# A dynamic convolution with a top-1 mixture of experts: PSUM tiles of three banks become tiles of two banks and of one, with a new order of the steps

## The chip, the core and the metric

The kernel runs on one core of a Trainium2 chip, with five engines: PE (TensorE, matmuls), DVE (VectorE), ACT (ScalarE), POOL (GpSimd) and SP (SyncE, here a queue of DMA issues). The metric is device time in microseconds of one execution; the median of three is quoted. TensorE's clock has two levels, 1.2 and 2.4 GHz; the profile gives the granted clock of a stretch as a share of the full one.

## What is computed

The reference has two stages. The first is a convolution whose seven weights per head come from a softmax of `weight_gen`; the second sends each row to the one expert with the largest logit.

```python
# batch 8, seq 3584, d_model 192, 8 heads of 24, K = 7
w = softmax(weight_gen, axis=-1)                       # [8, 3584, 8, 7]
x_pad = np.concatenate([zeros(8, 6, 192), x], axis=1)
out[b, s, h, g] = sum_k w[b, s, h, k] * x_pad[b, s + k, h, g]
# 28672 rows of 192; E = 8 experts, F = 1024
logits = out @ w_gate + modality_bias[modality_id]
e = argmax(logits); p = softmax(logits)[e]
y = p * (relu(out @ w1[e]) @ w2[e])
```

## The kernel before

**Units and pages.** The first stage works on 16 units u: 8 batches times 2 halves. A unit has 14 tokens on each of the 128 partitions, in two chunks c of 7 tokens, so a tap (one of 7 weights times the shifted x) is an operation on 128x1344. The second stage works on pages of 256 rows that belong to one expert (128 rows for the last five): 5 pages after unit 0, 7 after each later unit, 115 in all. After a unit's rows are known its gate, its route (which page and place each row gets) and the scatter of its rows to HBM follow; pages then load rows by expert.

**A page.** Rows and weights are held as two f16 parts (`hi` and `lo`). `page_h` (HM, L1021) makes half of the 1024 hidden columns at a time: two groups of 20 matmuls 128x256, each into 1024 f32 columns of PSUM. `page_hi` (HA, L1033, ACT) writes relu of it as f16, `page_lo` (HL, L1037, DVE) the remainder. `page_out` (OM, L1050 to L1052) makes the second product for half a page: 24 matmuls 128x192, which read both groups' `hi` and `lo` (tile `hl`). `page_store` (OA, L1057, ACT) scales that output by the gate's weight into `ot`, `page_scatter` (OS, L1062, POOL) sends it to `out`. `page_scale` (GM, L1006) prepares the scale.

**A unit.** `softmax_exp` (X, L532, ACT), sums on DVE, then `softmax_n` (BN, L562, DVE) writes the chunk's normalised weights `wn`, 392 columns, into PSUM. Each `tap` (PQ, L568, DVE) reads `wn` and writes a product, which `add` (PA, L619, DVE), `add_far` (DA, L614, an adding DMA that POOL issues) and `merge` (PM, L623) sum up. Units 0 and 1 take another way: `product` (M, L580) on DVE and `tap_sum` (S, L597), which sums on PE with an identity into a PSUM accumulator. `rows_hi` (H, L629, ACT) and `rows_lo` (L, L637 and L638, DVE) split the sum into f16 parts. `bias_rows` (XB, L536, ACT) copies the gate's bias for modality 0, `token_bias` (BP, L547, DVE) puts in that of modality 1. The gate's weights are prepared once: `gate_bound` (L432, DVE), `gate_parts` (L441 to L447) with `place` (L421).

**PSUM.** Two tiles hold nearly everything, `banks[0]` and `banks[1]`, three banks (1536 f32 columns) each. Columns 0 to 1023 take h: group 0 of each page in `banks[0]`, group 1 in `banks[1]`. The last bank of `banks[0]` takes the outputs of OM, its two halves by turns; the last bank of `banks[1]` takes `wn`. For units 0 and 1 a whole tile is the accumulator. Waits between engines are put in by the framework, which sees tiles.

**The order.** The program is one list, the string ORDER, of 3614 tokens such as `HM.45.0` (step, page or unit, part). Each token's step is issued in that order, so the list fixes the order on every engine's queue.

Of the kernel before, what the change touches and what calls it, by code (L numbers as in the profile page):

```python
# [1171 lines left out]
```

## Time and profile before

| what | value |
|---|---|
| median of 3 runs (lowest, highest) | 1463.68 us (1463.45, 1466.26) |
| the profiled execution | 1476.15 us |
| its span | 1474.4 us |
| busy: PE, DVE, ACT, POOL | 1186.4, 1018.2, 605.6, 575.3 us |
| mean granted clock of TensorE | 0.931 |

The span goes from the first to the last instruction of the one profiled execution; the rest of that execution's time lies around it. Busy time is the union of an engine's instructions. An engine's idle time is put down to the event that ended it (the releaser). Instructions are named by line and by tile: `hl<-banks` on L1037 reads a PSUM tile and writes `hl`.

### The profile page before, as it was taken

What the parts mean: (1) busy time and instruction counts of PE and PEld (TensorE: products, weight loads), DVE (VectorE), ACT (ScalarE), POOL (GpSimd) and SP (SyncE); (2) the same over time, 40 slices, a digit from 0 to 9 for tenths busy, and PEclk for the clock granted to TensorE, in tenths of its full rate; (3) what the DMA queues carried; (4) which work ended last, traced back from release to release, by engine and by line L of the source; (5) the groups of instructions that cost most, each with busy time, mean ns of one, the idle gap of its engine ahead of it and who ended that gap; (6) DMA issues with size and microseconds to landing.
All of it is one profiled execution on the core that took longest, in us unless ns stands there. A gap on an engine that the chain in (4) does not pass through costs nothing. (4 is left out here: it accounts for less than half of the span.)

```text
span 1474.4 us, 30152 instructions
## 1 busy us (share of the span) xinstructions
PE 1186.4 (80%) x11625; PEld 1035.1 (70%) x11625; DVE 1018.2 (69%) x1225; ACT 605.6 (41%) x1051; POOL 575.3 (39%) x566
## 2 busy tenths in 40 slices
PE   7587677788788888888878887888788888878884
PEld 3345566677777777777777777777677877768883
DVE  5687788887778786778867676678677878442210
ACT  3766353534435453534334362354234333323321
POOL 2151524352262625253534435126352534433111
PEclk8789889999999999999999899899899999989997
DMA  9577654796354565635464633548676463742122
GB/s 300 179 260 232 165 137 123 207 284 152 71 144 83 154 151 152 132 85 152 100 173 95 180 87 78 147 84 194 119 167 162 97 130 79 165 119 63 39 78 66
DMA packets 200630, 206.02 MB, mean 140 GB/s; under 512 B 157088, under 2 KB 173724, under 8 KB 195489
## 3 DMA queue, kind: packets, MB, share of 16 engines
q1 hardware_dynamic: 170720, 120.50, 30.8%
q0 software_dynamic: 29760, 83.53, 23.9%
q8 instruction: 93, 1.52, 0.4%
q14 instruction: 57, 0.47, 0.1%
HBM read 262.81 MB, written 57.95 MB: 218 GB/s over the span
## 5 line engine op out<-in xcount | busy, mean ns | idle before, releaser
L1021 PE MATMUL banks<-xT,w 128*128 128x256 f16 (+1 forms) x4600 | 548.2, 276 | 59.4 <-DVE hl L1037 18.7
L1050 PE MATMUL banks<-w,hl 128*128 128x192 f16 x1800 | 466.0, 259 | 153.9 <-DVE hl L1037 104.2
L1021 PEld LDWEIGHTS <-w 128*128 128x128 f16 x4600 | 448.0, 100 | 124.9 <-issue 49.5
L1062 POOL DMA_INDIRECT out_dram<-ot,meta x225 | 251.8, 1119 | 634.3 <-ACT ot L1057 391.2
L1052 PE MATMUL banks<-w,hl 128*128 128x192 f16 x1800 | 467.3, 260 | 3.4 <-DVE hl L1037 3.4
L1051 PE MATMUL banks<-w,hl 128*128 128x192 f16 x1800 | 467.1, 259 | 0.0
L1037 DVE SCALAR_TENSOR_TENSOR hl<-banks,hl 128x1024 f16<-128x1024 f32 x225 | 273.5, 1219 | 202.6 <-ACT ot L1057 107.8
L1033 ACT ACTIVATE hl<-banks 128x1024 f16<-128x1024 f32 x225 | 229.4, 1020 | 295.3 <-PE banks L1052 134.5
L743 POOL DMA_INDIRECT rows_scratch<-rows,idx x224 | 253.5, 1132 | 148.0 <-ACT rows L738 77.0
L1051 PEld LDWEIGHTS <-hl 128*128 128x128 f16 x1800 | 185.7, 103 | 175.2 <-issue 171.9
L568 DVE TENSOR_TENSOR shared<-banks,xt 128x1344 f32<-128x1344 f32 x140 | 216.4, 1550 | 80.1 <-PE banks L1021 72.1
L1057 ACT ACTIVATE ot<-banks,gm 128x192 f32<-128x192 f32 x225 | 93.6, 418 | 387.2 <-PE banks L1021 275.1
L1050 PEld LDWEIGHTS <-hl 128*128 128x128 f16 x1800 | 185.6, 103 | 10.2 <-ACT hl L1033 6.6
L1052 PEld LDWEIGHTS <-hl 128*128 128x128 f16 x1800 | 186.4, 104 | 6.7 <-DVE hl L1037 4.5
L619 DVE TENSOR_TENSOR shared<-shared 128x1344 f32<-128x1344 f32 x84 | 129.9, 1546 | 0.7
L568 DVE TENSOR_TENSOR prod<-banks,xt 128x1344 f32<-128x1344 f32 x56 | 86.8, 1551 | 36.4 <-PE banks L1021 33.1
L614 POOL DMA_DIRECT2D shared<-prod x56 | 54.0, 972 | 79.5 <-DVE prod L568 70.9
L597 PE MATMUL banks<-prod,ident 128*128 128x512 f32 x144 | 66.6, 616 | 20.9 <-DVE prod L580 13.6
L651 ACT ACTIVATE xg<-gt 128x768 f16<-128x768 f16 x84 | 67.6, 805 | 29.3 <-PE gt L647 28.6
L597 PEld LDWEIGHTS banks<-prod,ident 128*128 128x128 f32 x144 | 29.9, 216 | 53.5 <-issue 36.9
L647 PE MATMUL gt<-ident,rows 128*128 128x128 f16 x504 | 45.6, 226 | 23.1 <-ACT xg L651 11.8
L503 ACT ACTIVATE junk<-xt 128x1920 uint8<-128x1920 f32 x32 | 57.5, 1797 | 0.8 <-DMA xt<-in_x_dram 0.6
(142 smaller groups left out, 742.3 us busy)
## 6 DMA issues: line engine op xcount, KB each, us to landing
w<-weights_scratch SPq DMA_DIRECT2D x115, 1280.5 KB
w<-weights_scratch SPq DMA_DIRECT2D x230, 256.0 KB
shared<-prod POOLq DMA_DIRECT2D x56, 672.0 KB
xt<-in_x_dram SPq DMA_DIRECT2D x15, 1920.0 KB
weights_scratch<-w SPq DMA_DIRECT2D x8, 1280.5 KB
wt<-in_weight_gen_dram SPq DMA_DIRECT2D x16, 392.0 KB
out_dram<-ot,meta POOLq DMA_INDIRECT x225
rows_scratch<-rows,idx POOLq DMA_INDIRECT x224
```

The lines of the kernel that those rows point to most:

```text
L568: return nc.vector.tensor_tensor(to.rearrange("p t (h g) -> p t h g", h=H), win, xin, ALU.mult)
L597: nc.tensor.matmul(un[u]["psum", c][:, q], lhsT=ident32, rhs=un[u]["pr", c, k][:, q], start=(k == order[0]), stop=(k == order[-1]))
L619: return nc.vector.tensor_tensor(a, a, un[u]["tmp"], ALU.add)
L743: i = nc.gpsimd.indirect_dma_start(out=rows, out_offset=bass.IndirectOffsetOnAxis(ap=idx[:, j:j + 1], axis=0), in_=ri[:, j, 0:ROW // 2], i ...
L1021: nc.tensor.matmul(o, lhsT=wt[:, w0:w0 + P], rhs=xT[:, xi, :pt], start=(q * pt % 512 == 0 and j == 0), stop=(j == 4), skip_group_check=True)
L1033: return nc.scalar.activation(hi, pg["ps", grp], AF.Relu)
L1037: return nc.vector.scalar_tensor_tensor(lo, live[i]["ps", grp], 0.0, hi, op0=ALU.max, op1=ALU.subtract)
L1050: nc.tensor.matmul(ps, lhsT=hi, rhs=wt[:, w0:w0 + D], start=(f == 0), stop=False)
L1051: nc.tensor.matmul(ps, lhsT=hi, rhs=wt[:, w0 + D:w0 + 2 * D], start=False, stop=False)
L1052: nc.tensor.matmul(ps, lhsT=lo, rhs=wt[:, w0:w0 + D], start=False, stop=(f == NFT - 1))
L1057: nc.scalar.activation(ot, pg["out", t], AF.Copy, scale=pg["gm"][:, t:t + 1])
L1062: w = nc.gpsimd.indirect_dma_start(out=out, out_offset=bass.IndirectOffsetOnAxis(ap=pg["meta"][:, t, 1:2], axis=0), in_=pg["res", t], in_o ...
```

## The change

The three-bank tiles are replaced by `pairs[0..1]` (1024 columns, two banks) for h, and `singles[0..1]` (512 columns, one bank): `singles[0]` takes the outputs, its two halves at columns 0 and 256, `singles[1]` takes `wn`. Eight banks are laid out as before. The accumulator of units 0 and 1 is split: its first 5 tokens (WIDE) are in a pair, the last 2 in a single, so H and L run as two parts each, and `tap_sum` cuts its three matmuls at 512 and 960 columns. The seven operations of `gate_parts` run on DVE. The token `XB.0` goes from second place to behind `SA.0.1`, and ORDER is another one: the same tokens, of which 2245 stand in other places. The diff, cut; of ORDER it shows the first line and the place of `BN.9.0`, of before and of the change:

```diff
-ORDER = """A.0 XB.0 TE.0 RI.0 RI.1 wld.0 X.0 SM.0 CL SN.0 B.0 WP SA.0.0 M.0.0.0 M.0.0.1 S.0.0.0 SA.0.1 M.0.0.2 wld.1 CC S.0.0.1 SB.0
...
-PA.8.1.6 OA.42.1 SC.7.13 PW.46 HL.44.0 GM.46 OM.43.0 HA.44.1 OS.41.1 BN.9.0 BP.9 HL.44.1 OS.42.0 HM.45.0 OA.43.0 PQ.9.0.0
...
+ORDER = """A.0 RI.0 TE.0 RI.1 wld.0 X.0 SM.0 CL SN.0 B.0 WP SA.0.0 M.0.0.0 M.0.0.1 S.0.0.0 SA.0.1 M.0.0.2 wld.1 CC S.0.0.1 XB.0 SB.0
...
+OM.42.1 PA.8.1.6 LU.10 XB.10 OS.41.1 HA.43.1 SC.7.9 HL.43.1 HM.44.0 OA.42.1 PW.46 GM.46 BN.9.0 SC.7.10 PQ.9.0.0 SC.7.11
+OM.43.0 HA.44.0 PQ.9.0.1 OS.42.0 HM.44.1 HL.44.0 OA.43.0 SC.7.12 PQ.9.0.3 SC.7.13 OM.43.1 HA.44.1 PQ.9.0.4 OS.42.1 HL.44.1
...
-        wn = un[u]["wn", c] = banks[1][:, 1024:1024 + n * H * K].rearrange("p (t h k) -> p t h k", h=H, k=K)
+        wn = un[u]["wn", c] = singles[1][:, 0:n * H * K].rearrange("p (t h k) -> p t h k", h=H, k=K)
...
-            un[u]["psum", c] = banks[turn_of("acc", 2)]
-            un[u]["acc", c] = un[u]["psum", c][:, :n * D].rearrange("p (t d) -> p t d", d=D)
-        for j in range(0, n * D, 512):
-            q = slice(j, min(j + 512, n * D))
-            nc.tensor.matmul(un[u]["psum", c][:, q], lhsT=ident32, rhs=un[u]["pr", c, k][:, q], start=(k == order[0]), stop=(k == order[-1]))
+            q = turn_of("acc", 2)
+            un[u]["psum", c] = pairs[q], singles[q]
+            un[u]["acc", c] = [(0, WIDE, pairs[q][:, 0:WIDE * D].rearrange("p (t d) -> p t d", d=D)),
+                               (WIDE, n, singles[q][:, 0:(n - WIDE) * D].rearrange("p (t d) -> p t d", d=D))]
+        wide, rest = un[u]["psum", c]
+        for to, a, z in ((wide, 0, 512), (wide, 512, WIDE * D), (rest, WIDE * D, n * D)):
+            o = 0 if to is wide else WIDE * D
+            nc.tensor.matmul(to[:, a - o:z - o], lhsT=ident32, rhs=un[u]["pr", c, k][:, a:z], start=(k == order[0]), stop=(k == order[-1]))
...
+    def pieces(u, c):
+        acc = un[u]["acc", c]
+        return acc if isinstance(acc, list) else [(0, CHUNKS[c][1], acc)]
...
-        nc.scalar.activation(ri.bitcast(F16)[:, :, 0:D], un[u]["acc", c], AF.Copy, scale=un[u]["sx"])
+        for a, z, acc in pieces(u, c):
+            nc.scalar.activation(ri.bitcast(F16)[:, a:z, 0:D], acc, AF.Copy, scale=un[u]["sx"])
...
-        ps = pg["ps", grp] = banks[turn_of("g1", 2)][:, 0:1024]
+        ps = pg["ps", grp] = pairs[turn_of("g1", 2)]
...
-        o = 1024 + 256 * pool["turn"]
-        ps = pg["out", t] = banks[0][:, o:o + D]
+        o = 256 * pool["turn"]
+        ps = pg["out", t] = singles[0][:, o:o + D]
...
-    banks = [psg.tile([P, 3 * 512], F32, name=f"banks{q}") for q in range(2)]
+    pairs = [psg.tile([P, 1024], F32, name=f"pair{q}") for q in range(2)]
+    singles = [psg.tile([P, 512], F32, name=f"single{q}") for q in range(2)]
```

`rows_lo` loops over `pieces` in the same way, and `place` and `gate_parts` differ only in `nc.vector` for `nc.gpsimd`.

What the change does to the queues is seen in three places. The first is DVE around the weights of unit 8, chunk 0 (L562 before, L563 now; taps are L568 and L569, `hl` is L1037 and L1048). Each row is an instruction with the semaphores that it waits for. Before:

```order
L562 TENSOR_TENSOR banks1_167<-wt_5853,sm_7010 128x392 [waits DVE_49,Activation_49]
L1037 SCALAR_TENSOR_TENSOR hl_160<-banks1_167,hl_160 128x1024 [waits DVE_49]
L568 TENSOR_TENSOR shared_171<-banks1_167,xt_5852 128x1344 [waits DMAHW5_49]
L568 TENSOR_TENSOR prod_7114<-banks1_167,xt_5852 128x1344
L568 TENSOR_TENSOR shared_171<-banks1_167,xt_5852 128x1344
L568 TENSOR_TENSOR shared_171<-banks1_167,xt_5852 128x1344 [waits PE_49]
L1037 SCALAR_TENSOR_TENSOR hl_160<-banks0_166,hl_160 128x1024 [waits PE_49,Activation_49]
L1037 SCALAR_TENSOR_TENSOR hl_160<-banks1_167,hl_160 128x1024 [waits Activation_49]
L619 TENSOR_TENSOR shared_171<-shared_171 128x1344 [waits DVE_49]
L568 TENSOR_TENSOR prod_7219<-banks1_167,xt_5852 128x1344 [waits DMASW6_49]
L623 TENSOR_TENSOR shared_171<-shared_171 128x1344 [waits DMASW2_49]
L568 TENSOR_TENSOR shared_171<-banks1_167,xt_5852 128x1344 [waits DVE_49,PE_49]
```

and now:

```order
L563 TENSOR_TENSOR single1_169<-wt_5841,sm_6752 128x392
L569 TENSOR_TENSOR shared_173<-single1_169,xt_5840 128x1344 [waits DMAHW5_49,DVE_49]
L569 TENSOR_TENSOR prod_7037<-single1_169,xt_5840 128x1344
L1048 SCALAR_TENSOR_TENSOR hl_160<-pair0_166,hl_160 128x1024 [waits Activation_49]
L569 TENSOR_TENSOR shared_173<-single1_169,xt_5840 128x1344 x2
L1048 SCALAR_TENSOR_TENSOR hl_160<-pair1_167,hl_160 128x1024 [waits Activation_49]
L623 TENSOR_TENSOR shared_173<-shared_173 128x1344 [waits DVE_49]
L569 TENSOR_TENSOR prod_7160<-single1_169,xt_5840 128x1344 [waits DMASW4_49]
L1048 SCALAR_TENSOR_TENSOR hl_160<-pair0_166,hl_160 128x1024 [waits Activation_49]
L569 TENSOR_TENSOR shared_173<-single1_169,xt_5840 128x1344 [waits DVE_49]
L1048 SCALAR_TENSOR_TENSOR hl_160<-pair1_167,hl_160 128x1024 [waits Activation_49]
```

The taps read `single1` and wait for no matmul; `hl` waits for ACT alone; one `hl` stands after each tap or two.

The second is the start of ACT's queue, with the bias copy (`bt`), the first exponential (`wt`) and the two sums over x (`junk`). Before:

```order
L536 ACTIVATE bt_219<-bias_86 128x112 [waits DMAHW0_49]
L757 ACTIVATE tb_221<-ee0_152 1x4 [waits Pool_49]
L632 ACTIVATE rows0_72<-ids_130 128x14
L632 ACTIVATE rows1_73<-ids_130 128x14
L532 ACTIVATE wt_75<-wt_75 128x784 [waits DVE_49]
L543 ACTIVATE sm_229<-sm_229 128x112 [waits DVE_49]
L503 ACTIVATE junk_237,asum_236<-xt_74 128x1920 [waits DMAHW3_49,DMAHW2_49,DMAHW1_49]
L503 ACTIVATE junk_246,asum_236<-xt_74 128x1920 [waits DMAHW5_49,DMAHW6_49,DMAHW4_49,Activation_49]
```

and now:

```order
L641 ACTIVATE rows0_72<-ids_130 128x14 [waits Pool_49]
L768 ACTIVATE tb_222<-ee0_152 1x4 [waits Pool_49]
L641 ACTIVATE rows1_73<-ids_130 128x14
L533 ACTIVATE wt_75<-wt_75 128x784 [waits DMAHW0_49,DVE_49]
L544 ACTIVATE sm_229<-sm_229 128x112 [waits DVE_49]
L504 ACTIVATE junk_237,asum_236<-xt_74 128x1920 [waits DMAHW3_49,DMAHW2_49,DMAHW1_49]
L504 ACTIVATE junk_246,asum_236<-xt_74 128x1920 [waits DMAHW5_49,DMAHW6_49,DMAHW4_49,Activation_49]
L537 ACTIVATE bt_266<-bias_86 128x112 [waits DMAHW0_49]
```

The copy has moved from the head of the queue to behind the two sums.

The third is the preparation of the gate's weights. Before, in POOL's queue, up to the DMA that adds the far tap of unit 0:

```order
L441 TENSOR_SCALAR gate_ex_110<-gate_max_109 128x1 [waits DVE_49,Pool_49]
L442 TENSOR_SCALAR gate_ex_110<-gate_ex_110 128x1 [waits Pool_49]
L421 TENSOR_SCALAR gate_sb_111<-gate_ex_110 128x1 [waits Pool_49]
L421 TENSOR_SCALAR gate_sb_111<-gate_ex_110 128x1
L445 TENSOR_SCALAR wgf_107<-wgf_107,gate_sb_111 128x48 [waits Pool_49]
L446 CAST wg_112<-wgf_107 128x6x8 [waits Pool_49]
L447 TENSOR_TENSOR wg_112<-wgf_107,wg_112 128x6x8 [waits Pool_49]
L614 DMA w_3_164<-prod_318 128x1344 [waits DVE_49]
```

and now, in DVE's queue, between the gate's bound and the next product:

```order
L433 TENSOR_REDUCE gate_max_109<-w_3_164 128x1 [waits DMAHW6_49]
L442 TENSOR_SCALAR gate_ex_110<-gate_max_109 128x1 [waits DVE_49]
L443 TENSOR_SCALAR gate_ex_110<-gate_ex_110 128x1 [waits DVE_49]
L422 TENSOR_SCALAR gate_sb_111<-gate_ex_110 128x1 [waits DVE_49]
L422 TENSOR_SCALAR gate_sb_111<-gate_ex_110 128x1
L446 TENSOR_SCALAR wgf_107<-wgf_107,gate_sb_111 128x48 [waits DVE_49,Pool_49]
L447 CAST wg_112<-wgf_107 128x6x8 [waits DVE_49]
L448 TENSOR_TENSOR wg_112<-wgf_107,wg_112 128x6x8 [waits DVE_49]
L581 TENSOR_TENSOR w_3_164<-xt_74,wt_75 128x1344 [waits DMAHW5_49,DMAHW4_49]
```

POOL's queue goes from the copies of the gate's weights (L439) straight to that DMA.

## Rows read from the trace of the kernel before

**Rows 1.** The view by stretches, with its line of columns, four of six stretches.
```profile
core 0: us, PE busy (x) PEld busy (x) DVE busy (x) ACT busy (x) POOL busy (x), PEclk, DMA share, GB/s
0.00:121.00 121.00, 88.48 (x339) 43.99 (x339) 84.71 (x97) 65.46 (x110) 39.17 (x75) 0.84 0.71 234
121.00:298.00 177.00, 130.18 (x1275) 112.78 (x1274) 146.99 (x170) 93.13 (x155) 66.67 (x60) 0.91 0.64 180
298.00:1302.00 1004.00, 832.17 (x8576) 754.29 (x8575) 742.22 (x890) 402.82 (x709) 425.90 (x386) 0.95 0.57 134
...
1340.00:1420.00 80.00, 70.22 (x721) 63.99 (x719) 20.22 (x17) 23.75 (x41) 15.48 (x16) 1.00 0.26 64
```

**Rows 2.** Waits of PE, 298 to 1302 us: us in total, times, longest us.
```profile
PE banks L1050 <- DVE hl L1037: 81.8, 57, 2.8
PE banks L1050 <- ACT ot L1057: 38.0, 63, 3.1
PE banks L1021 <- DVE hl L1037: 13.1, 10, 1.4
PE banks L1021 <- DVE shared L568: 9.0, 11, 2.1
```

**Rows 3.** Waits of ACT and DVE, 298 to 1302 us.
```profile
ACT ot L1057 <- PE banks L1021: 219.1, 62, 6.7
...
ACT hl L1033 <- PE banks L1052: 106.1, 60, 3.8
...
DVE shared L568 <- PE banks L1021: 68.2, 24, 10.0
...
DVE hl L1037 <- ACT ot L1057: 30.8, 26, 3.0
```

**Rows 4.** Timeline near 605 us: start, us, what, [idle before it <- releaser].
```profile
604.25 1.56 DVE L568 TENSOR_TENSOR shared<-banks,xt 128x1344 f32<-128x1344 f32 x1 [2.43 <-PE banks L1021]
...
607.58 2.34 PE L1021 MATMUL banks<-xT,w 128*128 128x256 f16 x20 [1.39 <-DVE hl L1037]
```

**Rows 5.** Waits of PE, 121 to 298 us.
```profile
PE banks L1050 <- DVE hl L1037: 15.8, 6, 3.1
...
PE banks L1021 <- ACT ot L1057: 5.3, 6, 2.5
```

**Rows 6.** Waits of PE, 1302 to 1420 us.
```profile
PE banks L1050 <- ACT ot L1057: 6.9, 11, 1.8
PE banks L1050 <- DVE hl L1037: 6.1, 11, 0.6
PE banks L1021 <- DVE hl L1037: 5.6, 1, 5.6
```

**Rows 7.** Timeline of the first 50 us: ACT, DVE, POOL, DVE.
```profile
13.12 0.30 ACT L536 ACTIVATE bt<-bias 128x112 f32<-128x112 f32 x1 [11.03 <-DMA bias<-n_moe_modality_bias_dram]
...
13.63 0.84 ACT L532 ACTIVATE wt<-wt 128x784 f32<-128x784 f32 x1
...
5.50 0.98 DVE L528 TENSOR_TENSOR wt<-wt,mx 128x784 f32<-128x784 f32 x1
...
33.80 5.78 POOL L441 TENSOR_SCALAR gate_ex<-gate_max 128x1 f32<-128x1 int32 x1 [19.03 <-DVE gate_max L432]
...
42.70 1.13 POOL L614 DMA_DIRECT2D w<-prod  x1
...
48.17 1.56 DVE L580 TENSOR_TENSOR prod<-xt,wt 128x1344 f32<-128x1344 f32 x1 [5.37 <-DMA w<-prod]
```

**Rows 8.** Two lines' instructions: duration ns min/median/max, first and last start us, forms.
```profile
L731 DVE TENSOR_TENSOR nbase<-nbase,lg x15: 101/103/104, 151.0 to 1309.5; 128x8 f32<-128x8 f32 x15
...
L686 DVE TENSOR_TENSOR L<-L,gmx x16: 264/275/276, 78.7 to 1302.1; 128x112 f32<-128x112 f32 x16
```

**Rows 9.** Lines of ACT, 298 to 1302 us: xcount, busy us, mean ns, idle before.
```profile
L1033 ACT ACTIVATE hl<-banks 128x1024 f16<-128x1024 f32 x172 | 175.4, 1020 | 223.8 <-PE banks L1052 106.1 <-DVE shared L568 59.0 <-PE banks L1021 22.3
...
L1057 ACT ACTIVATE ot<-banks,gm 128x192 f32<-128x192 f32 x172 | 71.8, 418 | 287.1 <-PE banks L1021 219.1 <-PE banks L1052 49.7 <-DVE hl L1037 9.7
```

More of the change, by code (lines that the diff above doesn't have):

```diff
@@ L45 @@
 ALWAYS = 5
+WIDE = 5
 FIRST = 2
@@ L285, in plan @@
+HL.112.0 GM.114 OS.110.0 OM.111.0 HM.114.0 HA.113.0 OA.111.0 HL.113.0 OS.111.0 OM.112.0 HA.114.0 OA.112.0 HL.114.0 OM.113.0
+OS.112.0 OA.113.0 OM.114.0 OS.113.0 OA.114.0 OS.114.0"""
 def plan():
@@ L419, in place @@
     def place(o, ex, sign, a):
[L421 removed]
+        nc.vector.tensor_scalar(o, ex, float(sign), float(a << 23) - sign * ROUND, op0=ALU.mult, op1=ALU.add)
     def put(o, ex, sign, a):
@@ L440, in gate_parts @@
     def gate_parts():
-        nc.gpsimd.tensor_scalar(gex, gmx.bitcast(I32), FLOOR, ROUND, op0=ALU.add, op1=ALU.add)
-        nc.gpsimd.tensor_scalar(gex, gex, ROUND + float(24 << 23), None, op0=ALU.max)
+        nc.vector.tensor_scalar(gex, gmx.bitcast(I32), FLOOR, ROUND, op0=ALU.add, op1=ALU.add)
+        nc.vector.tensor_scalar(gex, gex, ROUND + float(24 << 23), None, op0=ALU.max)
         place(gsb[:, 0:1], gex, -1, 263)
         place(gsb[:, 1:2], gex, 1, -9)
-        nc.gpsimd.tensor_scalar(wgf, wgf, gsc[:, 0:1], None, op0=ALU.mult)
-        nc.gpsimd.tensor_copy(wg[:, :, 0, :], wgf)
-        nc.gpsimd.tensor_tensor(wg[:, :, 1, :], wgf, wg[:, :, 0, :], ALU.subtract)
+        nc.vector.tensor_scalar(wgf, wgf, gsc[:, 0:1], None, op0=ALU.mult)
+        nc.vector.tensor_copy(wg[:, :, 0, :], wgf)
+        nc.vector.tensor_tensor(wg[:, :, 1, :], wgf, wg[:, :, 0, :], ALU.subtract)
     desc = const.tile([P, E], F32, name="desc")
@@ L635, in rows_lo @@
         c0, n = CHUNKS[c]
-        acc, sx, rw = un[u]["acc", c], un[u]["sx"], rbuf[u % NR][:, c0:c0 + n, :].bitcast(F16)
-        nc.vector.scalar_tensor_tensor(rw[:, :, D:D + 64], acc[:, :, P:D], sx, rw[:, :, P:D], op0=ALU.mult, op1=ALU.subtract)
-        nc.vector.scalar_tensor_tensor(rw[:, :, 256:384], acc[:, :, 0:P], sx, rw[:, :, 0:P], op0=ALU.mult, op1=ALU.subtract)
+        sx = un[u]["sx"]
+        for a, z, acc in pieces(u, c):
+            rw = rbuf[u % NR][:, c0 + a:c0 + z, :].bitcast(F16)
+            nc.vector.scalar_tensor_tensor(rw[:, :, D:D + 64], acc[:, :, P:D], sx, rw[:, :, P:D], op0=ALU.mult, op1=ALU.subtract)
+            nc.vector.scalar_tensor_tensor(rw[:, :, 256:384], acc[:, :, 0:P], sx, rw[:, :, 0:P], op0=ALU.mult, op1=ALU.subtract)
     def gate_a(u, j):
```

438 lines of the change are left out of this document (217 added, 221 removed).

## The prediction

> **What bounds the kernel now.** I read the profile in stages first, because the mean over the span (PE busy 80%) mixes parts with different limits. The view by stretches [rows 1] cuts the span at 121 us (the first page's first matmul), 298 us (route of unit 3), 1302 us (route of unit 15) and 1340 us. The stretch from 298 to 1302 us is what the kernel repeats: 12 units of attention beside 12 times 7 pages of experts, 1004 us, 83.7 us a unit. There PE is busy 832.2 us and DVE 742.2 us, ACT 402.8. No engine is full, DMA is at 0.57, and PE is idle for 1004 - 832.2 = 171.8 us. So the next question is what ends PE's idle time.
>
> The view of waits, for PE in that stretch [rows 2], answers it: 81.8 + 38.0 + 13.1 + 9.0 = 141.9 us of the 171.8 end with another engine giving back a buffer or finishing half a page: DVE with `hl` (L1037), ACT with `ot` (L1057), DVE with a tap (L568). The gate and the weights' DMA have the small rest.
>
> Then I asked why DVE and ACT are late, in the waits of those engines [rows 3]. ACT's `ot` (L1057, a read of the second product's output) waits 219.1 us for L1021, which is the *first* product of another page and has nothing to do with `ot`. ACT's `hl` (L1033) waits 106.1 us for L1052, the second product of an older page. DVE's taps (L568, which read the softmax weights) wait 68.2 us for L1021. None of these is a flow of data. What the pairs have in common is a tile: `banks[0]` holds the first group's h in columns 0 to 1023 and both outputs behind them, `banks[1]` the other group's h and the softmax weights `wn`. Whoever writes any part of a tile waits for whoever reads any other part, and the reverse. The timeline shows one turn [rows 4]: at 604.25 a tap starts after 2.43 us of waiting for an L1021 group; the `hl` behind it in DVE's queue starts late; and PE's next L1021 group, at 607.58, has waited 1.39 us for that `hl`. A false wait on one engine so comes back to PE as a true one.
>
> **The change, part by part.**
>
> *Tiles.* h gets `pairs[0..1]` (two banks each), the outputs `singles[0]`, `wn` `singles[1]`. The same number of operations of the same shapes runs per page, so nothing is added in the main stage. What goes: the waits of L1057 for L1021, of L1033 for L1052, of L568 for L1021 and L1033, of L1021 for L568 and L1057. The two pieces of DVE's queue shown with the change say so: of six taps of unit 8 two waited for PE, in the new order none does, and L1037 has lost its waits for PE. What stays is true: the second product needs both `lo` halves, a group of h needs its pair read by L1037, and, because both outputs lie in one tile still, the second product waits for the `ot` before it.
>
> How much of the 141.9 us goes? Upper end: all of it. Lower end: DVE's queue is in order and carries 742.2 us of work in any case; with taps of 1.5 us ahead of an L1037 some lateness stays. The 38.0 on `ot` and the 9.0 on taps, a third of the sum, fall with what made those late; of the 81.8 + 13.1 on `hl` goes what came through `ot`, L1052 and the taps, of which the view names 30.8 us on L1037 directly [rows 3], though not all of that reaches PE. I set the low end at 40%, 57 us. I take two thirds, 95 us, because in the chain of [rows 4] the true wait at its end is wholly due to the false one at its head. What is left is 1004 - 95 = 909 us for 832.2 us of PE work, 92% busy, and from 1340 to 1420 us, with DVE almost free, PE was 88% busy with 13 us of these waits in it.
>
> *Clock.* In the main stage the granted clock is 0.95, in the stretch 1340 to 1420 it is 1.00 with 70.2 us busy of 80 [rows 1]. Shorter gaps should give part back. If all came back, 832.2 x 0.05 = 41.6 us of PE time go; at worst nothing. I take half: 20 us. Main stage: -95 - 20 = -115 us, bounds -57 and -183.
>
> *The first pages, 121 to 298.* PE waits 15.8 us for `hl` on L1050 and 5.3 for `ot` on L1021 [rows 5], 21.1 in all. But DVE is busy 147.0 us of 177, with the softmax, the route and the weights' splitting: it is nearer to a bound than PE (130.2). I take a third, -7; bounds 0 and -21.
>
> *End of the main work, 1302 to 1420.* PE's waits are 6.9 for `ot`, 6.1 for `hl` on L1050 and 5.6 on L1021 [rows 6]. The first two, 11 times each, are the ring through `banks[0]`: `ot` waits for L1021, `hl` for `ot`. They go, -13; the 5.6 is one wait for the last route, which is true. Bounds -7 (only `ot`'s share) and -19. The last 54 us wait for weights and stay: 0.
>
> *Start, 0 to 121.* Three edits meet here. **The bias copy** stands second in ACT's queue and waits 11.03 us for its DMA; the exponential (L532) behind it starts at 13.63, though DVE gave its input at 5.50 + 0.98 = 6.48 [rows 7]. Moved behind the two `junk` sums, it frees up to 13.63 - 6.5 = 7.1 us for the exponential; DVE's first products need x as well, which lands in between at a time no row gives. Bounds 0 and -7, I take -3.5. Who needs the copy (the bias of the gate) comes much later, so its new place costs nothing; were the scales behind it late, that would cost its 0.30 us. **The gate's parts**: POOL makes seven of them from 33.80 on, the first alone 5.78 us, and issues the DMA that adds the far tap only at 42.70; DVE waits 5.37 us for that DMA at 48.17 [rows 7]. On DVE the same seven take between 7 x 0.103 and 7 x 0.275 us by the nearest small rows [rows 8], 0.7 to 1.9; I take 1.2, near the middle, since their forms lie between 128x1 and 128x48. POOL's queue then has the DMA next, as its order shows, and DVE's 5.37 us goes in large part: net between +1.9 (something else ends the wait) and -4.7; I take -3. **The split accumulator** of units 0 and 1 doubles the eight DVE parts of the rows and the four on ACT: eight more DVE operations at 0.103 to 0.275 us above what the columns take, 0.8 to 2.2 us, and DVE is busy 84.7 of 121 us. I take +1; its matmuls stay three a tap (512, 448 and 384 columns where there were 512, 512 and 320). Sum -5.5, bounds +4 and -12.
>
> *New order.* The same steps in other places. I price it at nothing by itself: the sizes above already suppose an order that suits the tiles. In the changed DVE queue the `hl` stand one after each one or two taps; that is the cover on which the two thirds rest, and if it is worse, rival B is the price.
>
> **Sum** on the profiled execution: -115 - 7 - 13 - 5.5 = -140.5 us; 1476.15 - 140.5 = 1335.65 us. That execution lies 0.85% over the median of the three runs (1463.68), so the forecast is 1335.65 x 1463.68 / 1476.15 = **1324 us**. A measurement of this kernel can tell about 0.2%.
>
> One rule speaks against the size. The row is the 38.0 us of L1050 for `ot` [rows 2], beside the 219.1 us that `ot` itself sat waiting for L1021 [rows 3]: by the rows `ot` is late because of a tile that it no longer shares, and most of the 38.0 goes. The Trainium skill, PSUM — Partial Sum Buffer, section "PSUM bank collisions raise a hardware error", asks that two engines be kept apart by bank, also where they touch different columns; by that the two outputs in one bank keep PE and ACT taking turns, and if all 38.0 us stayed, two thirds of it, 25 us, would be missing: 1349 us. The trace of before cannot show a one-bank output.
>
> **Rivals.**
> - **B: DVE's queue is the bound.** Taps stand ahead of `hl` in order, and DVE's 742.2 us in 909 would be 82% busy with 12 dependent rounds a unit. Then only 40% goes and the clock stays at 0.95: -57 - 13 - 5.5 = -75.5, 1401 on the profile, 1389 us. For it: the largest wait on PE is `hl` (81.8). Against: ACT and DVE are themselves held by PE for more than that [rows 3].
> - **C: PE gets packed.** All waits and the whole clock: -183 - 14 - 9 - 13 = -219, 1257, so 1246 us. For it: the 1.00 clock at 88% busy. Against: the main stage has route, gate and DVE work that the tail lacks. On the side of C, the Trainium skill, TensorE: Matmul & The Clock Gate, Part 1, says that the slow clock is the default and that activity lifts it; the trace agrees (0.95 where PE is 83% busy with long gaps, 1.00 in the tail).
> - **D: slower, by ACT.** Each of 225 second products now waits for the `ot` of the one before, on one tile. If ACT's queue has an `hl` of 1.020 us ahead of each `ot` (0.418 us) [rows 9] and that `hl` is not ready, PE waits at each: up to 225 x 1.02 = 230 us, which outweighs the 140: 1476 + 230 - 140 = 1566, 1552 us. It decides where `ot` starts later than one group of L1021 (2.34 us [rows 4]) less 0.42, some 1.9 us, after the second product ends. Against it: ACT is busy only 402.8 of 1004 us. That rule of the Trainium skill's PSUM page, named above, would keep this wait.
> - **E: the change doesn't do what it says.** If the false waits only stand in front of true ones that end at the same time, the gain is lost and the time stays near 1464. Against: `ot` on L1021 cannot be true anywhere.
>
> **How the numbers follow.** The forecast (A) has 0.66, alone from 1285 to 1365 (one half to nearly all of the waits, clock nothing to most). B 0.19, C 0.08, D 0.04, E 0.03. Range 1265 to 1400: it leaves out C, D, E and the far edge of B. Faster by over 0.2%: A, B and C, 0.93; within 0.2%: E, 0.03; slower: D, 0.04.
>
> **What would show it.** In the changed profile the rows `ot` <- L1021 (219.1), `hl` <- L1052 (106.1) and L568 <- L1021 (68.2) should be all but gone; PE's 81.8 and 38.0 should fall to about a third; the unit's period from 83.7 to some 74 us; the clock from 0.95 to 0.97; the exponential should start before 13 us and the far tap's DMA before 40 us. I am wrong if L1050 <- `ot` grows (D), if L1050 or L1021 <- `hl` stays with DVE over 85% busy (B), or if the three rows vanish and the period doesn't move (E).

## The result, and the profile after

The changed kernel takes 1262.51 us (median of 4 runs, 1260.26 to 1270.25) against 1463.57 us (4 runs, 1460.35 to 1466.26): the ratio is 0.8636, 95% interval 0.8595 to 0.8678. It is faster, as forecast, but by 201 us where 140 were forecast, and the time lies 2.5 us below the range. The profiled execution took 1263.99 us, its span is 1262.2 us.

The same cuts as before, made at the same events (first page, route of unit 3, route of unit 15), give this:

| stretch | before | after | measured | forecast |
|---|---|---|---|---|
| to the first page's first matmul | 121.3 | 116.4 | -4.9 | -5.5 |
| from there to the route of unit 3 | 176.6 | 160.6 | -16.0 | -7 |
| route of unit 3 to route of unit 15 | 1004.6 | 831.3 | -173.3 | -115 |
| from there to the end | 172.0 | 153.9 | -18.1 | -13 |

The view by stretches of the changed kernel, with its line of columns, shows the two inner stretches and the two after them:

```profile
core 0: us, PE busy (x) PEld busy (x) DVE busy (x) ACT busy (x) POOL busy (x), PEclk, DMA share, GB/s
116.00:277.00 161.00, 126.38 (x1286) 108.05 (x1285) 150.54 (x175) 93.38 (x155) 70.95 (x60) 0.95 0.71 199
277.00:1108.00 831.00, 772.35 (x8557) 723.25 (x8555) 727.38 (x888) 407.20 (x707) 421.53 (x385) 0.97 0.71 159
1108.00:1146.00 38.00, 35.25 (x368) 33.10 (x367) 16.92 (x47) 12.73 (x23) 21.42 (x22) 0.96 0.51 149
1146.00:1214.00 68.00, 65.89 (x680) 61.70 (x678) 19.60 (x16) 24.06 (x41) 14.57 (x15) 0.97 0.27 71
```

Beside [rows 1], in the long stretch PE's idle time fell from 171.8 to 831 - 772.4 = 58.6 us, by 113. PE's *busy* time fell too, from 832.2 to 772.4, by 59.8 us, for the same work. DVE's work stayed (742.2 and 727.4 us) and is now 88% of the stretch. The unit takes 69.3 us where it took 83.7.

PE's waits in that stretch, beside [rows 2]:

```profile
PE single L1061 <- ACT ot L1068: 36.1, 12, 12.0
PE pair L1032 <- DMA xT<-rows_scratch: 9.8, 1, 9.8
PE lg L719 <- DVE oh L708: 3.8, 3, 2.5
PE pair L1032 <- DMA w<-weights_scratch: 3.0, 2, 2.4
```

Of the four rows of before, three are gone altogether: `hl` on the second product (81.8), `hl` on the first (13.1), taps (9.0). The fourth, the second product waiting for `ot`, is still 36.1 us, but in 12 times, the longest 12.0 us, where it was 63 times of at most 3.1.

The waits of ACT and DVE, beside [rows 3]:

```profile
ACT hl L1044 <- PE pair L1032: 149.1, 107, 4.3
ACT ot L1068 <- PE single L1063: 102.1, 105, 3.0
DVE hl L1048 <- ACT hl L1044: 87.2, 31, 11.1
ACT gm L1017 <- DMA w<-weights_scratch: 79.2, 29, 9.2
...
ACT gm L1017 <- DMA meta<-rows_scratch: 31.9, 6, 10.7
```

Every one of these is a flow of data: `hl` waits for the product that it reads, `ot` for the last matmul of its own output (L1063), L1048 for the `hi` that it subtracts, and `gm` for two loads. `ot` <- first product (219.1) and tap <- first product (68.2) don't appear, and of `hl` <- second product (106.1) 3.0 us are left. In their place two rows of ACT have grown: the page's scale (`gm`, L1017) waits 79.2 us for weights (35.4 in this stretch before) and 31.9 for a page's `meta`.

The timeline at the longest wait shows what these two rows do. First SP's queue, then ACT, then PE:

```profile
934.38 10.07 SPq L983 DMA_TRANSPOSE xT<-rows_scratch  x1
944.72 0.55 SPq L985 DMA_DIRECT2D meta<-rows_scratch  x1
...
952.26 0.30 ACT L1017 ACTIVATE gm<-meta,w 128x2 f32<-128x2 f32 x1 [10.74 <-DMA meta<-rows_scratch]
952.46 1.79 ACT L504 ACTIVATE junk<-xt 128x1920 uint8<-128x1920 f32 x1
...
954.25 0.40 ACT L1068 ACTIVATE ot<-single,gm 128x192 f32<-128x192 f32 x1
...
940.16 0.25 PE L1062 MATMUL single<-w,hl 128*128 128x192 f16 x1
940.24 0.25 PE L1063 MATMUL single<-w,hl 128*128 128x192 f16 x1
...
954.70 0.32 PE L1061 MATMUL single<-w,hl 128*128 128x192 f16 x1 [12.03 <-ACT ot L1068]
954.81 0.36 PE L1062 MATMUL single<-w,hl 128*128 128x192 f16 x1
954.97 0.36 PE L1063 MATMUL single<-w,hl 128*128 128x192 f16 x1
```

A transposing load of a later page takes 10.07 us on SP's queue, and the load of `meta` stands behind it. `gm` of that later page stands in ACT's queue ahead of an `ot` of an earlier page (in ORDER, `GM.83` ahead of `OA.80.0`), so `ot` starts at 954.25 and the second product has waited 12.03 us. Matmuls then come to start 0.16 us apart; before the pause they went at 0.08. The granted clock was 1.00 before the pause and is 0.50 behind it: it fell to its lower level while PE stood still.

### The profile page after: what moved, and what is told of

It reads as the page before. It is cut to its first block, busy times and chain, and to the rows that moved or that the text cites. A ratio compares the mean times of both kernels' runs of the same rounds, so it can differ in the third digit from the quotient of the medians.

```text
span 1262.2 us, 30221 instructions
## 1 busy us (share of the span) xinstructions
PE 1117.4 (89%) x11625; PEld 999.8 (79%) x11625; DVE 1008.9 (80%) x1240; ACT 614.0 (49%) x1055; POOL 580.3 (46%) x559
## 5 line engine op out<-in xcount | busy, mean ns | idle before, releaser
L1032 PE MATMUL pair<-xT,w 128*128 128x256 f16 (+1 forms) x4600 | 537.5, 273 | 25.5 <-DMA w<-weights_scratch 15.3
L1061 PE MATMUL single<-w,hl 128*128 128x192 f16 x1800 | 453.3, 252 | 48.8 <-ACT ot L1068 46.1
L1063 PE MATMUL single<-w,hl 128*128 128x192 f16 x1800 | 453.5, 252 | 9.5 <-DVE hl L1048 9.5
L1062 PE MATMUL single<-w,hl 128*128 128x192 f16 x1800 | 453.4, 252 | 0.0
L1048 DVE SCALAR_TENSOR_TENSOR hl<-pair,hl 128x1024 f16<-128x1024 f32 x225 | 273.5, 1217 | 187.9 <-ACT hl L1044 184.0
L1044 ACT ACTIVATE hl<-pair 128x1024 f16<-128x1024 f32 x225 | 229.2, 1018 | 224.0 <-PE pair L1032 206.6
L754 POOL DMA_INDIRECT rows_scratch<-rows,idx x224 | 260.5, 1163 | 131.3 <-ACT rows L749 59.8
L1062 PEld LDWEIGHTS <-hl 128*128 128x128 f16 x1800 | 180.4, 100 | 52.8 <-issue 50.1
L569 DVE TENSOR_TENSOR shared<-single,xt 128x1344 f32<-128x1344 f32 x140 | 215.7, 1549 | 0.5
L1063 PEld LDWEIGHTS <-hl 128*128 128x128 f16 x1800 | 180.6, 100 | 13.1 <-DVE hl L1048 12.2
L1061 PEld LDWEIGHTS <-hl 128*128 128x128 f16 x1800 | 180.4, 100 | 6.3 <-ACT hl L1044 3.4
L1068 ACT ACTIVATE ot<-single,gm 128x192 f32<-128x192 f32 x225 | 93.7, 416 | 154.1 <-PE single L1063 145.5
L1017 ACT ACTIVATE gm<-meta,w 128x2 f32<-128x2 f32 (+1 forms) x115 | 33.4, 290 | 135.0 <-DMA w<-weights_scratch 100.1
L569 DVE TENSOR_TENSOR prod<-single,xt 128x1344 f32<-128x1344 f32 x56 | 86.7, 1548 | 0.0
L618 POOL DMA_DIRECT2D shared<-prod x56 | 54.4, 990 | 57.7 <-DVE prod L569 42.9
L601 PE MATMUL pair<-prod,ident 128*128 128x512 f32 (+1 forms) x96 | 49.0, 637 | 13.0 <-DVE prod L581 10.5
```

The source lines that it names most:

```text
L569: return nc.vector.tensor_tensor(to.rearrange("p t (h g) -> p t h g", h=H), win, xin, ALU.mult)
L754: i = nc.gpsimd.indirect_dma_start(out=rows, out_offset=bass.IndirectOffsetOnAxis(ap=idx[:, j:j + 1], axis=0), in_=ri[:, j, 0:ROW // 2], i ...
L1032: nc.tensor.matmul(o, lhsT=wt[:, w0:w0 + P], rhs=xT[:, xi, :pt], start=(q * pt % 512 == 0 and j == 0), stop=(j == 4), skip_group_check=True)
L1044: return nc.scalar.activation(hi, pg["ps", grp], AF.Relu)
L1048: return nc.vector.scalar_tensor_tensor(lo, live[i]["ps", grp], 0.0, hi, op0=ALU.max, op1=ALU.subtract)
L1061: nc.tensor.matmul(ps, lhsT=hi, rhs=wt[:, w0:w0 + D], start=(f == 0), stop=False)
```

## Experiments

Two theories stood against each other. Theory 1: waits for other parts of the same tile are the cost, and giving each use its own tile removes it in nearly any order. Theory 2: the new order is what gains, and the tiles only allow it. Kernels that ran side by side share a chip and the runs of the kernel before. **The chip of the first four was slower for all**: the kernel before took 1650.66 us there. Their ratios are used, and the same kernels were run again elsewhere. Where an expectation is in us, the ratio times 1464 us is held against it.

**tiles_alone, tiles_again.** The new tiles on the old order, the gate's parts on POOL.

```diff
-ORDER = """A.0 RI.0 TE.0 RI.1 wld.0 X.0 SM.0 CL SN.0 B.0 WP SA.0.0 M.0.0.0 M.0.0.1 S.0.0.0 SA.0.1 M.0.0.2 wld.1 CC S.0.0.1 XB.0 SB.0
+ORDER = """A.0 XB.0 TE.0 RI.0 RI.1 wld.0 X.0 SM.0 CL SN.0 B.0 WP SA.0.0 M.0.0.0 M.0.0.1 S.0.0.0 SA.0.1 M.0.0.2 wld.1 CC S.0.0.1 SB.0
...
-        nc.vector.tensor_scalar(gex, gmx.bitcast(I32), FLOOR, ROUND, op0=ALU.add, op1=ALU.add)
+        nc.gpsimd.tensor_scalar(gex, gmx.bitcast(I32), FLOOR, ROUND, op0=ALU.add, op1=ALU.add)
```

Expected of the first:

> The kernel before with the new PSUM tiles alone: its own order, the gate's parts on POOL, the bias copy second. Theory 1 (tile-wide waits are the cost, whatever the order): the rows ot <- L1021, hl <- L1052 and L568 <- L1021 fall below 30 us each and most of the gain is here, 1290 to 1340 us. Theory 2 (the order carries the gain, the tiles only allow it): the three rows fall too, but hl stays behind the taps where the old order put it, and the time is 1380 to 1450 us.

Of the second, on another chip:

> The new tiles alone on the old order, beside the changed kernel. On the first chip the ratio was 0.874. Theory 1 (tiles carry most): 0.87 to 0.90 here, the rest, 1 to 4 per cent, is the order's. Theory 2 (the order carries most): 0.92 to 0.97 on this chip.

Measured: 0.8737 (0.8683 to 0.8792) on the slow chip, 1439.09 us; 0.880 (0.877 to 0.883) on the other, 1291.28 us against 1466.84. Of the second, the long stretch, PE's waits and ACT's in it:

```profile
287.00:1137.60 850.60, 782.24 (x8578) 729.03 (x8579) 732.18 (x892) 406.12 (x711) 443.22 (x386) 0.97 0.69 159
...
PE single L1061 <- ACT ot L1068: 29.3, 16, 5.8
...
PE pair L1032 <- DVE hl L1048: 9.3, 5, 4.7
...
ACT hl L1044 <- PE single L1062: 57.8, 25, 3.5
...
ACT hl L1044 <- PE single L1063: 14.0, 11, 2.7
```

The stretch takes 850.6 us, 154 less than before, with the order untouched; `hl` ahead of PE has shrunk from 81.8 + 13.1 to 9.3. Theory 1 holds: of the 196.6 us that the whole change gains on the same chip, the tiles alone gain 175.6. (0.8737 of 1464 is 1279 us, 11 below the range that theory 1 gave.)

One of the three rows that it named did not fall as expected. `ot` and the taps wait for no first product any more, but `hl` <- second product, expected under 30 us, is 57.8 + 14.0 = 71.8 where it was 106.1. In the old order this is a true wait: all 60 waits of that row before, and all 36 here, are of a page's first `hl` for the last second product of the page two before, and `hl` has two turns, so the one writes over what the other still reads. The shared tile only made it longer, from the last matmul that reads this half of `hl` (L1062) to the last of the product. In the old order a page's first group of h stands ahead of that second product in 91 of 110 pages, in the new order in 5. With the new order on shared tiles (the next experiment) the row is still 112.8 us, but 57 of its 60 waits are for the page just before, of which nothing is written over: these are false. Only tiles and order together bring the row to 3.0.

One thing is worse: the first page begins at 127.5 us instead of 121.3 (at 126.3 on the slow chip). Up to there the split accumulator is the only edit that bears, so this is its price in the old order, some 6 us; two profiles of the changed kernel differ by 3 there (116.4 and 119.6).

**order_alone, order_again.** The kernel before with the new order and nothing else.

```diff
-ORDER = """A.0 XB.0 TE.0 RI.0 RI.1 wld.0 X.0 SM.0 CL SN.0 B.0 WP SA.0.0 M.0.0.0 M.0.0.1 S.0.0.0 SA.0.1 M.0.0.2 wld.1 CC S.0.0.1 SB.0
+ORDER = """A.0 RI.0 TE.0 RI.1 wld.0 X.0 SM.0 CL SN.0 B.0 WP SA.0.0 M.0.0.0 M.0.0.1 S.0.0.0 SA.0.1 M.0.0.2 wld.1 CC S.0.0.1 XB.0 SB.0
...
```

> The kernel before with the new order alone, on the three-bank tiles, the gate's parts on POOL. Theory 1: the order was made for free tiles; with shared ones each first product stands between an output and its read, so the three rows grow and the time is 1440 to 1560 us. Theory 2: part of the gain is the order's own, 1330 to 1420 us.

> The new order alone on the three-bank tiles, beside the changed kernel. On the first chip the ratio was 0.964. Theory 1: 0.97 to 1.05. Theory 2: 0.91 to 0.96.

Measured: 0.9636 (0.9591 to 0.9681), 1593.21 us on the slow chip, and 0.9704 (0.9666 to 0.9742), 1424.02 us. The order gains 43 us on the shared tiles. Theory 1's second range only just holds that; its first (1440 to 1560) missed, and 0.9636 of 1464, 1411 us, lies in the first range of theory 2. So the order has a part of its own, but the smaller one; the late bias copy is in these 43 us (its own price is below). PE's waits from 288.5 to 1249.9 us, second run:

```profile
PE banks L1050 <- ACT ot L1057: 58.2, 90, 4.0
PE banks L1021 <- DVE shared L568: 26.6, 19, 2.8
PE banks L1050 <- ACT hl L1033: 24.6, 19, 5.7
PE banks L1050 <- DVE hl L1037: 9.4, 8, 4.0
```

`hl` (DVE) fell from 81.8 to 9.4, so the order does place `hl` better; `ot` rose from 38.0 to 58.2 and the taps from 9.0 to 26.6, which are the false waits that this order was not made for.

**after_again.** The changed kernel unaltered, beside these.

> The changed kernel unaltered, as the reference of this call: the first four experiments ran on a chip on which the kernel before took 1650 us instead of 1464. If both kernels scale alike the ratio is 0.864 again; if the slower chip punishes waits, and the changed kernel has fewer, the ratio there is lower, 0.80 to 0.84.

Measured: 0.8654 (0.8608 to 0.8701), 1270.25 us against 1466.84, the same ratio as the result's. (It ran on a chip of the usual speed, so what the slow chip makes of the changed kernel stays open.) Over the tiles alone, order, gate and bias copy together add 1291.28 - 1270.25 = 21 us.

**out_with_h, wn_with_h, and both again.** The changed kernel with one of the two old sharings put back.

```diff
-    pairs = [psg.tile([P, 1024], F32, name=f"pair{q}") for q in range(2)]
-    singles = [psg.tile([P, 512], F32, name=f"single{q}") for q in range(2)]
+    joined = psg.tile([P, 3 * 512], F32, name="joined")
+    pairs = [joined[:, 0:1024], psg.tile([P, 1024], F32, name="pair1")]
+    singles = [joined[:, 1024:1536], psg.tile([P, 512], F32, name="single1")]
```

The other of the two, with the same `joined`, has instead

```diff
+    pairs = [psg.tile([P, 1024], F32, name="pair0"), joined[:, 0:1024]]
+    singles = [psg.tile([P, 512], F32, name="single0"), joined[:, 1024:1536]]
```

> The changed kernel, but the outputs' bank lies in one tile with the first group's h, as before; the softmax weights keep their own. Both theories: ot waits for the first product again. If the outputs' tile is the larger part of the false waits, 1380 to 1470 us; if the weights' tile is, 1270 to 1330 us.

> The changed kernel, but the softmax weights' bank lies in one tile with the second group's h, as before; the outputs keep their own. DVE's taps wait for the first product again (68.2 us before). If the outputs' tile is the larger part, 1290 to 1340 us; if the weights' tile is, 1380 us or more. The two losses should add up to more than 150 us, unless one wait hides the other.

> As out_with_h, on another chip, beside the changed kernel's ratio 0.865. The first chip gave 0.935. Theory (a tile's false waits cost about the same share on either): 0.92 to 0.95, so the outputs' own tile is worth 80 to 125 us.

> As wn_with_h, on another chip. The first chip gave 0.908. Theory: 0.89 to 0.92, so the weights' own tile is worth 40 to 80 us, and both together are about what the new order alone lacks (0.970 less 0.865, 154 us). If they are far apart from that sum, the two waits hide one another.

Measured: outputs with h 0.9354 (0.9302 to 0.9406) and 0.9467 (0.9428 to 0.9507, 1384.49 us); weights with h 0.9084 (0.9051 to 0.9116) and 0.9091 (0.9057 to 0.9124, 1331.22 us). Against the changed kernel's 0.865 the outputs' own tile is worth 0.9467 - 0.8654 = 0.081, some 119 us, the weights' own tile 0.044, some 64 us, both within the second ranges. (The first expectation for the outputs missed by a little: 0.9354 of 1464 is 1369 us, 11 under its range.) The sum, 183 us, is more than the 154 us between the order alone and the whole, so the two hide one another in part, by some 30 us (by the four intervals, 12 us either way). The waits of the second runs in the long stretch, outputs with h first (ACT, then PE), then weights with h:

```profile
ACT ot L1068 <- PE joined L1032: 183.3, 64, 6.4
...
ACT hl L1044 <- PE joined L1063: 111.0, 59, 4.6
...
PE joined L1061 <- ACT ot L1068: 68.3, 102, 3.5
...
ACT hl L1044 <- DVE shared L569: 98.1, 31, 5.5
...
PE joined L1032 <- DVE shared L569: 34.7, 24, 3.4
DVE shared L569 <- PE joined L1032: 22.5, 19, 2.5
```

Each sharing brings back its own rows. With the outputs, `ot` waits 183.3 us for the first product again (219.1 in [rows 3]) and `hl` 111.0 for the second, nearly all of them false ones for the page just before. With the weights, `hl` waits 98.1 us for taps (59.0 in [rows 9]) and taps 22.5 for the first product (68.2).

**gm_late.** The changed kernel with each page's scale moved to directly ahead of that page's first `ot`.

```diff
-PA.10.1.5 OM.55.1 PL.60 HA.56.1 SC.9.4 A.11 SC.9.5 HM.57.0 OA.55.1 PW.59 GM.59 HL.56.1 X.11 SC.9.6 PQ.10.1.6 OM.56.0 SC.9.7
+OA.55.0 SC.9.3 PA.10.1.5 OM.55.1 PL.60 HA.56.1 SC.9.4 A.11 SC.9.5 HM.57.0 OA.55.1 PW.59 HL.56.1 X.11 SC.9.6 PQ.10.1.6 OM.56.0
...
-OM.59.0 GM.62 RA.10.5 HA.60.0 RA.10.6 RB.10.0 PA.11.0.5 SE.10 RR.10 HL.60.0 OA.59.0 HM.60.1 OS.59.0 RB.10.1 RB.10.2 RB.10.3
+RA.10.5 HA.60.0 RA.10.6 RB.10.0 PA.11.0.5 SE.10 RR.10 HL.60.0 GM.59 OA.59.0 HM.60.1 OS.59.0 RB.10.1 RB.10.2 RB.10.3 RB.10.4
```

> The changed kernel with each page's scale (GM, L1017) moved in the order to directly ahead of that page's first ot. In the changed kernel the second product's longest waits (12.0 us at 954 us, 6.5 at 667) are for an ot that stands in ACT's queue behind a GM, and that GM waits for the next page's DMA. Theory (ACT's queue, in order, is what is left): the row L1061 <- ot falls from 46.1 to under 12 us and the time by 20 to 40 us against the changed kernel. Rival (the DMA itself is late, and the wait only moves to L1032 for w or xT): less than 8 us.

Measured: 1226.38 us (1220.15 to 1232.37), ratio 0.836 (0.8316 to 0.8403), 44 us under the changed kernel on the same chip, a little more than the 20 to 40 expected: a version that beats both. The long stretch and PE's waits in it:

```profile
278.80:1083.80 805.00, 767.03 (x8563) 719.75 (x8561) 728.14 (x890) 410.42 (x706) 427.25 (x385) 0.98 0.74 164
...
PE single L1058 <- ACT ot L1065: 11.1, 8, 3.9
...
PE pair L1029 <- DMA xT<-rows_scratch: 9.6, 1, 9.6
PE pair L1029 <- DMA w<-weights_scratch: 3.8, 1, 3.8
```

(Line numbers are three lower in this kernel.) `ot` ahead of PE fell from 36.1 to 11.1 us, over the whole span from 46.1 to 22.7, which is more left than the 12 expected; the DMA's own lateness did not take its place (9.6 and 3.8 us). The stretch takes 805 us, 67.1 a unit, PE 95% busy. So 25 of the 36.1 us came from ACT's queue, in order, behind a load; in this stretch the one tile that both outputs share can account for 11.1 us of PE's idle time at most.

**gate_pool, bias_first.** The changed kernel one with the gate's parts on POOL again, one with the bias copy second again. The first:

```diff
-        nc.vector.tensor_scalar(gex, gmx.bitcast(I32), FLOOR, ROUND, op0=ALU.add, op1=ALU.add)
+        nc.gpsimd.tensor_scalar(gex, gmx.bitcast(I32), FLOOR, ROUND, op0=ALU.add, op1=ALU.add)
...
```

and the other

```diff
-ORDER = """A.0 RI.0 TE.0 RI.1 wld.0 X.0 SM.0 CL SN.0 B.0 WP SA.0.0 M.0.0.0 M.0.0.1 S.0.0.0 SA.0.1 M.0.0.2 wld.1 CC S.0.0.1 XB.0 SB.0
+ORDER = """A.0 XB.0 RI.0 TE.0 RI.1 wld.0 X.0 SM.0 CL SN.0 B.0 WP SA.0.0 M.0.0.0 M.0.0.1 S.0.0.0 SA.0.1 M.0.0.2 wld.1 CC S.0.0.1 SB.0
...
```

> The changed kernel with the gate's parts back on POOL. Theory (the prediction's): the far tap's DMA starts some 9 us later again and DVE waits up to 5 us for it, so 3 to 6 us more than the changed kernel, the ratio to before 0.867 to 0.870. Rival: the first page's start hangs on the route and its scatter (POOL), not on that DMA; the new order alone, with the gate on POOL, began its first page at 117.4 us, the changed kernel at 116.4 and 119.6; then within 2 us.

> The changed kernel with the bias copy back in second place. The exponential, at 6.2 us in the changed kernel, starts at 13 us again. Theory: DVE's first products are late by the same 6 to 7 us and all behind them, 4 to 7 us more, ratio 0.868 to 0.872. Rival: the first page waits for loads of weights or for POOL, and the 7 us are absorbed before 116 us: within 2 us.

Measured: the gate on POOL 0.8643 (0.861 to 0.8675), 1264.25 us, which is no difference that these runs can tell (the interval is 5 us to either side). The bias copy early 0.8749 (0.8717 to 0.8781), 1283.52 us: against the 0.8643 beside it 0.0106 more, some 15 us (the medians lie 19 apart), and the two intervals don't meet. That is two to three times the 4 to 7 us expected. Of the gate on POOL, POOL's rows, and DVE's wait for the far tap's DMA in the changed kernel:

```profile
24.82 1.38 POOL L442 TENSOR_SCALAR gate_ex<-gate_max 128x1 f32<-128x1 int32 x1 [3.27 <-DVE gate_max L433]
...
31.58 1.13 POOL L618 DMA_DIRECT2D w<-prod  x1
...
42.98 1.56 DVE L581 TENSOR_TENSOR prod<-xt,wt 128x1344 f32<-128x1344 f32 x1 [4.82 <-DMA w<-prod]
```

The first of the seven takes 1.38 us here, not the 5.78 of [rows 7]; the DMA is issued at 31.58 instead of 28.87 in the changed kernel; and with the parts on DVE the wait for that DMA is still 4.82 us, at 42.98. With the parts on POOL, and the DMA issued later, DVE has no such wait; in the same stretch it waits 2.82 us for ACT (L638) and 2.12 and 0.51 for PE (L601) instead. Of the early bias copy (lines three lower), ACT's first rows, and the same two of the changed kernel:

```profile
12.21 0.29 ACT L534 ACTIVATE bt<-bias 128x112 f32<-128x112 f32 x1 [10.10 <-DMA bias<-n_moe_modality_bias_dram]
...
12.72 0.84 ACT L530 ACTIVATE wt<-wt 128x784 f32<-128x784 f32 x1
...
6.19 0.86 ACT L533 ACTIVATE wt<-wt 128x784 f32<-128x784 f32 x1
...
13.68 0.28 ACT L537 ACTIVATE bt<-bias 128x112 f32<-128x112 f32 x1
```

The exponential is 6.5 us later, and the first page begins at 128.2 us instead of 116.4 to 119.6: nothing between absorbs the delay. How 6.5 us become 9 to 12 there and some 15 in all was not followed.

## Why the prediction was right in direction and wrong in size

**The mechanism held.** The three rows named as false waits are gone, the order shown for DVE and ACT does what it says, and 0.880 with the tiles alone shows that the tiles, not the order, carry most of it. But one of the three was misread as "none of these is a flow of data": `hl` <- second product (106.1) was a true wait for a buffer, which the tile made longer. 71.8 us of it stay with the tiles alone, and the new order, priced at nothing, is what took them. So rival E (the waits only stand in front of true ones) is right for that row, and refuted for the time. Rival B (DVE's queue keeps 60% of the waits) too: the view of PE's waits has no row for `hl` in the long stretch, with DVE 88% busy, over the 85% that the text named. Rival D needed `ot` to hold PE up at each second product; it does so 12 times. The outcome is nearest to C, 1246 us. (C's last three terms, 14, 9 and 13, are less than the bounds of 21, 12 and 19 given for those parts; with the bounds it would have been 1231.)

**The step that failed is the main stage's sum, -95 - 20 = -115 us, where 173 us went: 113 us of PE's idle time and 60 of its busy time. The second term was wrong the most.** The first: "I take two thirds, 95 us" of 141.9. The same rows now hold 36.1 us, so 105.8 went; and those 36.1 are not what I left them for (lateness of `hl` behind taps), but a wait that I had not named, `gm` ahead of `ot`. Of what I had in view nearly all went: with the scale moved, 11.1 + 0.4 us of it are left. The argument against taking it all, that a full DVE queue keeps `hl` late, was wrong: PE's waits for `hl` are gone, and with the old order too no more than 9.3 us were left. A reason can be worked out, though no run isolates it: in the new order (`HM.44.1 ... OM.43.1 ... HM.45.0 ... OM.44.0`) a second product and a first one stand between a group and the product that needs its `hl`: 24 x 0.082 + 2.34 = 4.3 us, against 1.02 + 1.22 for the two halves of `hl`, so a tap of 1.55 us ahead of it still fits.

The second: "*Clock.* ... I take half: 20 us". PE's busy time fell by 59.8 us, more than the 41.6 that I had called all of it. Two things are in that. One is the clock, which I had priced by the wrong product: the stretch's mean of 0.95 times all of PE's busy time. What counts is how long PE is busy at the lower level, where matmuls go at 0.16 us instead of 0.08 and half the time is lost. Added up over the stretches with a granted clock of 0.50, that was 102.8 us before and is 33.5 now; half of the difference, 34.6 us, is the clock's.

The other I had left out, the ends of matmuls. A matmul that is followed by another gives way after 0.08 us, but the profile lets it run 0.25 us to its end, and counts those 0.17 us as busy where nothing follows. (The profile models these ends; but an `ot` that waits for the last matmul of its output starts 0.28 us after that matmul's start, so the time does pass.) The view of waits lists 164 waits of PE in the long stretch before and 25 after, so 139 x 0.17 = 24 us. 34.6 and 24 make 58 of the 59.8 us.

Two pairs of runs tell the parts apart. The outputs with h and the scale late are busy at the lower level for nearly the same time, 25.9 and 23.3 us, but have 158 and 25 waits: busy 790.5 and 767.0 us, and 133 x 0.17 = 22.6 of those 23.5 us are the ends of matmuls. The kernel before and the outputs with h have nearly the same number of waits, 164 and 158, but 102.8 and 25.9 us at the lower level: busy 832.2 and 790.5, 42 us, of which half of 76.9, 38 us, is the clock. The outputs' row:

```profile
276.60:1197.60 921.00, 790.53 (x8562) 721.69 (x8560) 733.44 (x889) 402.44 (x707) 422.62 (x385) 0.98 0.63 143
```

All kernels in order of PE's idle time in the long stretch:

| kernel | PE idle us | PE busy us |
|---|---|---|
| before | 172 | 832 |
| new order alone | 154 | 808 |
| outputs with h | 130 | 791 |
| weights with h | 101 | 786 |
| tiles alone | 68 | 782 |
| the change | 59 | 772 |
| the change, scale late | 38 | 767 |

From first to last, 134 us less of idle time go with 65 us less busy.

**The first pages, -16.0 against -7.** I took a third of PE's 21.1 us because DVE was nearer to a bound. It was, and is busy 150.5 of 161 us now; but then DVE's own idle time was the row to read, and that fell from 177 - 147 = 30 to 10.5 us. **The end, -18.1 against -13.** The `hl` and `ot` waits of [rows 6], 13.0 together, are 4.9 us now; the one of 5.6 us on the last route, which I had called true, is gone as well. Up to the cut at 1420 us (1214 now) that makes some 12 us. The other 6 fell in the last stretch, 54.4 us before and 48.2 now, for which I had taken 0.

**The start, -4.9 against -5.5: right by wrong parts.** The gate's parts, for which I took -3, are worth nothing that the runs can tell: DVE waits as long in that stretch either way, for the DMA or for ACT and PE, which was near my upper bound. The bias copy, for which I took -3.5 within 0 and -7, is worth some 9 to 12 us at the first page and 15 in all, outside my bound: I took the delay of the exponential for the most that can follow. The split accumulator, for which I took +1, costs about 6 us where it stands alone (127.5 against 121.3). Equal sums were luck.

**The wait for `ot`, 38.0 us in [rows 2].** By the rows most of it should have gone; the figure of 1349 us had all of it stay, because both outputs lie in one bank. It stayed, at 36.1, which looks as if the bank had done it; but the run with the scale late leaves 11.1, so 25 of the 36.1 had another cause, and the bank can have at most the rest. The Trainium skill (PSUM — Partial Sum Buffer, "PSUM bank collisions raise a hardware error") asks that engines be kept apart by bank; no run here has the two outputs in two banks, so what that would give stays open.

## What to carry to other kernels

Where a releaser in the waits doesn't produce what the waiting instruction reads, look for a tile that both touch in different parts, and give each use its own; here that alone was worth 12%, with the order unchanged. Look first whether the releaser reads what the waiting instruction overwrites: then the wait is true, and only another order or one buffer more can move it. Price a wait of TensorE at more than its idle time: over these kernels each microsecond of idle time that went took about half a microsecond of busy time with it. And in an engine's queue put an instruction that waits for a DMA no earlier than its result is needed: moving 115 of them was worth 44 us more.

## What the runs showed of the hardware that was not expected

One chip ran the same kernels 11 to 13% slower (before 1650.66 us against 1464, the tiles alone 1439.09 against 1291.28), with the same duration of an operation (1.22 us for `hl` on both) but other waits and a lower granted clock (0.909 against 0.945 for the tiles alone). The tiles alone on that chip, PE's waits over the span:

```profile
PE pair L1032 <- issue: 59.2, 70, 4.5
PE single L1061 <- ACT ot L1068: 36.9, 24, 4.6
PE single L1061 <- issue: 27.1, 20, 10.0
```

PE stood 59.2 and 27.1 us in which it waited for nothing that the profile shows; on the other chip those rows don't appear. The ratios to the kernel before agree all the same to within 0.012: 0.874 and 0.880, 0.964 and 0.970, 0.935 and 0.947, 0.908 and 0.909. What held PE there was not found, nor whether the lower clock is its cause or its effect.
